# DeltaNet and an MLP on one core: the first MLP product in 15 block products instead of 11 of 12, joins on four tiles, and a new planned order

## The chip, the cores and the metric

The kernel runs on one core of a Trainium2 chip. Its time is the device time of that core in microseconds (us), the median over the runs. A core has five engines, each with an in-order queue: PE (TensorE matmuls; their weight loads are listed apart as PEld), DVE (VectorE), ACT (ScalarE), POOL (GpSimd) and SP (SyncE, which here only issues DMAs). POOL issues DMAs too.

## The reference

All in float32, with B = 4, H = 8, S = 768, D = 48:

```python
k_n = k / (norm(k) + 1e-6)
state = zeros((B, H, D, D))
for t in range(S):                                   # DeltaNet, per batch and head
    y[:, :, t] = einsum('bhd,bhde->bhe', q[:, :, t], state)
    v_old = einsum('bhde,bhd->bhe', state, k_n[:, :, t])
    state += beta[:, :, t] * einsum('bhd,bhe->bhde', k_n[:, :, t], v[:, :, t] - v_old)
x = y.transpose(0, 2, 1, 3).reshape(B, S, H * D)     # (4, 768, 384)
xn = (x - mean) / sqrt(var + 1e-6) * g_ln
out = x + maximum(xn @ w_ch1, 0) @ w_ch2             # 384 -> 1536 -> 384
```

## The kernel before, in words

*Chunks.* The sequence is cut into 12 chunks of 64 steps. Within a chunk the recurrence becomes matrix work for all 32 (batch, head) pairs: Gram matrices of the keys, the inverse of a triangular 64x64 matrix per pair, and then products with the state. After the recurrence of chunk c (`recur`) its 256 tokens (64 steps of 4 batches) go through LayerNorm and the MLP (`mlp(c)`). The chunks depend on each other through the state alone; the MLPs are free to lag behind.

*Inverse.* `rows_inverse` treats two chunks at once. The Gram matrix goes out to DRAM (tile `gd`), comes back by eight DMAs as `gb` with one 32x32 block per partition, is inverted row by row on DVE into `xb` (two operations per row, L1045 and L1050, over the scratch tile `tmp`), goes out to DRAM again (`xd`), and comes back by eight DMAs as the diagonal blocks of `xt`. Chunk 1 has 16x16 blocks and an extra step, `blocks_join` (L1077, L1082: 128 small products, matrices of 32 rows and 32 columns at four positions of the array). Then `join(c)` makes the off-diagonal 32x32 block of each 64x64 inverse: a transposed copy `xnj` on DVE, product E (L1110), a negated copy `es` on ACT, product Z (L1115), and a copy into `xt` on ACT. Each product is 32 matmuls, alternating between two positions of the array; the copies are two of 512 columns.

*Recurrence.* Per chunk PE makes the products with the keys and queries (L963), the state's products (L1160), u (L1215), y (L1222) and the state's update (L1232), each about 1 us. The turn of y into tokens, the LayerNorm and the transposes into `xnt` follow.

*MLP.* The first product is 384 -> 1536 for 256 tokens, the second 1536 -> 384. Chunks 0, 1 and 2 (c < FROM = 3) make the first product plainly: 12 tiles of three matmuls of 256 columns (L1483). From chunk 3 on it goes through `eleven`: with the inputs in three blocks, the hidden units in two halves, and the tokens in two halves, 11 block products replace 12. Each block product is three slabs of two matmuls of 128 columns (L1416). It needs five mixes of token blocks per chunk on POOL (L1397) and, once, sums of blocks of the weights on POOL (`sums_of_w1`, L1372), three into the buffers `q_` and two in place. DVE adds the PSUM banks into the hidden tiles (L1438), ACT copies and applies relu (L1432, L1435). The second product from chunk 1 on is `seven`: 7 block products in place of 8 (L1584), with combinations of the hidden blocks on POOL (L1570, L1609). Filler products on zeros (L1662) keep PE busy where nothing else is ready at the start.

*Order.* Nothing runs where it is written. Each operation is recorded as a Step with a cost, the buffers it reads and writes, and a priority; a list scheduler (class `Line`, `run`) plans start times with modelled costs, and every engine's queue is then issued in the planned order. MLP products on PE carry a due time, taken from a table:

```python
DUE = [44.40, 70.70, 90.32, 129.22, 162.45, ...]     # one entry for each chunk, then slopes
def due(c, t): return DUE[c] + DUE[12 + min(c, 2)] * t
```

A product with a due time yields to small recurrence work unless its due time is close (URGENT, STALL). HOP, GIVE, PATIENCE, SLACK and EAGER are further constants of the planner. The order in which the parts are recorded breaks ties:

```python
prep_x(1); mlp(0); ...; prep_g(2); prep_x(2)
for c in range(2, NCH):
    step(c)                  # loads, norms, queries, join, recurrence of chunk c
    mlp(c - 1)
    if c % 2 and c + 3 < NCH: prep_g((c + 3) // 2); prep_x((c + 3) // 2)
mlp(NCH - 1)
```

All DMAs go through one helper (L555), on SP's queue or on POOL's.

Of the kernel before, what the change touches and what calls it, by code (L numbers as in the profile page):

```python
# [16 lines left out]
C = 64  # L17
DP = 64
# [47 lines left out]
PASS = 0.0165  # L66


class Step:
    __slots__ = (  # L70
        "eng", "cost", "fn", "deps", "pr", "lag", "bulk", "start", "end", "n", "users", "name", "t0", "np", "arr", "hold", "ready", "least", "due", "port", "banks"
# [3 lines left out]
class Line:  # L75
# [17 lines left out]
    def add(self, eng, cost, fn, r=(), w=(), pr=0.0, lag=0.0, bulk=None, name="", t0=0.7, after=(), np=0, arr=0.0, hold=None, due=None, port=0):  # L93
# [3 lines left out]
        s.hold, s.due = False, due  # L97
# [137 lines left out]
    def run(self):  # L235
# [47 lines left out]
        while todo:  # L283
            best = None
            for e in ENGS:
                for rd, s in self.avail[e]:
                    t = when(s, e, rd)
                    if t is not None and (best is None or t < best[0]):
                        best = (t, e)
# [4 lines left out]
            t, e = best  # L294
# [32 lines left out]
            s.start = t  # L327
            if e in ports:
                ports[e] = (t + s.cost, s.port)
# [3 lines left out]
            if s.bulk is not None:  # L333
                free[e] = t + s.cost
                self.dma_go(t)
                self.sent["sw" if e == "Pool" else "hw"].append(s)
                self.rings[e].append([s, max(s.bulk, 1e-6), t + s.cost + self.DMA_ISSUE])
                continue
# [5 lines left out]
            else:  # L344
                free[e] = s.end = t + s.cost
# [10 lines left out]
    def schedule(self):  # L356
# [5 lines left out]
        for s in reversed(every):  # L362
# [3 lines left out]
            s.pr = min(late + [s.due if s.due is not None else 1e6])  # L366
# [31 lines left out]
def kernel(  # L398
# [47 lines left out]
    NH = 14  # L446
# [46 lines left out]
    half_w = DFF // 2  # L493
    second = [t.rearrange("p h t -> p (h t)") for t in (qts[1], pts[1])]
    q_ = [second[0][:, 0:half_w], second[1][:, 0:half_w], sb("q_last", [128, half_w])]
    d_ = [t[:, half_w + 128 * i : half_w + 128 * i + 128] for t in second for i in range(2)] + [ident]
# [258 lines left out]

    def fill(n, cols, ps, pk, after=(), **kw):
# [257 lines left out]
    def rows_inverse(L, chunks, beta_l, xd, **kw):  # L1014
        gv, xv = (t.rearrange("p s t -> p (s t)")[:, 0 : L * L].rearrange("p (s t) -> p s t", t=L) for t in (gb, xb))
        gbk = [("gb", n) for n in range(8)]
        nb, ns = GH * L, 13.7 if L == BK else 11
        add("Pool", 0.1 + 0.85e-3 * L * L, lambda: nc.gpsimd.memset(xv, 0.0), [], ["xb"], after=MASK_SCRATCH, **kw)
        for n, (p0, c, rows, cols) in enumerate(spots(L, chunks)):
            dma(  # L1020
                "SP", gv[p0 : p0 + GH], gds[c % NG][rows, :, cols].rearrange("s h t -> h s t"),
                nb, ns, [("gd", c % NG)], [("gb", n)], **kw,
# [11 lines left out]
        add("Pool", 0.25, lambda: nc.gpsimd.tensor_copy(out=diag(xv), in_=db), ["db_b"], ["xb"], **kw)  # L1034
# [5 lines left out]
        for j in range(L - 1):  # L1040
            n, w = j + 1, L - 1 - j

            def row(j=j, n=n, w=w):
                t = tmp[:, 0 : n * w].rearrange("p (s t) -> p s t", t=w)
                nc.vector.tensor_tensor(  # L1045
                    out=t, in0=xv[:, 0:n, j : j + 1].to_broadcast([128, n, w]),
                    in1=gv[:, j : j + 1, j + 1 : L].to_broadcast([128, n, w]), op=ALU.mult,
                )
                rest = xv[:, 0:n, j + 1 : L]
                nc.vector.tensor_tensor(out=rest, in0=rest, in1=t, op=ALU.subtract)  # L1050
# [3 lines left out]
        dma("SP", xdv, xv, 128, 25 + L * L * 0.15, ["xb"], [("xd", xd)], **kw)  # L1054
        for n, (p0, c, rows, cols) in enumerate(spots(L, chunks)):
            if L < BK:
# [3 lines left out]
                nb, ns, [("xd", xd), ("xz", c % NX)], [("xq", c % NX, n % 8 if L < BK else n % 4)], **kw,  # L1060
            )

    def blocks_join(c, **kw):
# [5 lines left out]
        XN, ES = ([(n, 0), (n, 1)] for n in ("xn", "es"))  # L1069
# [14 lines left out]
        pe(128, prod_e, gk + XN, ATT, 0.22, **kw)  # L1084
        add("ACT", act(512), lambda: nc.scalar.mul(es, pe_, -1.0), ATT, ES, **kw)
        pe(128, prod_z, ES + xq + XT, BY[:2], 0.22, **kw)
# [6 lines left out]
    def xt_keys(c):  # L1093
        return [("xq", c % NX, n) for n in range(8)] + [("xz", c % NX)] + [
            (n, c % NX, g) for n in ("xt", "xo") for g in range(2)
        ]

    def join(c, **kw):
# [7 lines left out]

        def prod_e():
            for h in range(GH):
                for e in range(2):
                    nc.tensor.matmul(p[quad(2 * e + 1), h], gs[quad(2 * e), h, BK:C], xnj[quad(2 * e), h])  # L1110

        def prod_z():
            for h in range(GH):
                for e in range(2):
                    nc.tensor.matmul(p[quad(2 * e), h], es[quad(2 * e + 1), h], xt[quad(2 * e + 1), h, c0 : c0 + BK])  # L1115

        pe(64, prod_e, gk + [("xn", 0), ("xn", 1)], [ATT[1]], 0.11, name=f"e{c}", **kw)
        for e in range(2):
            rows = quad(2 * e + 1)
            add("ACT", act(512), lambda rows=rows: nc.scalar.mul(es[rows], p[rows], -1.0), [ATT[1]], [("es", e)], **kw)  # L1120
        pe(64, prod_z, [("es", 0), ("es", 1)] + xq, [ATT[0]], 0.11, name=f"z{c}", **kw)
        for e in range(2):
            rows = quad(2 * e)
            add(
                "ACT", act(512), lambda rows=rows: nc.scalar.copy(xt[rows, :, BK:C], p[rows]),
                [ATT[0]], [("xo", c % NX, e)], **kw,
# [678 lines left out]
```

## Time and profile before

| what | value |
|---|---|
| median of 3 runs | 560.05 us (558.03 to 564.31) |
| span of the profiled execution | 559.0 us, 1.05 below the median of the runs |
| busy: PE / DVE / ACT / POOL | 525.5 / 370.3 / 192.1 / 253.2 us |
| first product, chunks 3 to 11 (L1416) | 648 matmuls of 128x128 |
| second product, chunks 1 to 11 (L1584) | matmuls of 128x192 |
| PE idle up to 175 us / from there to 460 us | 26 us / about 3 us |

A row of the timeline reads: start, length, engine, line, operation, output and inputs by the program's names, tile shape and count; a bracket at its end is the idle time of the engine just before, and what ended it. PE's counts in the timeline are records, of which a float32 matmul has two. A row of the groups has shapes, count, busy time, mean ns of one, and idle time before.

### The profile page before, as it was taken

To read this page: it belongs to the slowest core of one execution; us is meant where nothing else is said; L and a number is where in the kernel's file an instruction comes from. 1 tells how busy PE (TensorE), PEld (TensorE's weight loads), DVE (VectorE), ACT (ScalarE), POOL (GpSimd) and SP (SyncE) were. 2 spreads that over 40 slices of the span, in tenths; PEclk is the share of its full clock that TensorE was granted. 3 is DMA by queue.
4 is the path that set the end of the run, shared out by engine and by line. 5 is a ranking of instruction groups with operands and counts; after the bars stand their busy time and mean duration, and the time that the engine had idled before them with its cause. 6 is when DMAs were issued, how large, how long until landed. Compare 5 with 4: busy or idle time off the path is not lost.

```text
span 559.0 us, 23060 instructions
## 1 busy us (share of the span) xinstructions
PE 525.5 (94%) x10060; PEld 478.8 (86%) x10060; DVE 370.3 (66%) x884; ACT 192.1 (34%) x452; POOL 253.2 (45%) x399
## 2 busy tenths in 40 slices
PE   7668869899998999899999999999999999999996
PEld 4547657678987899899999999999999999999996
DVE  5666549991689936889858968668777436253331
ACT  5667644232232324232323332513322224323030
POOL 5252337407885656267270352452352522426242
PEclk9898899999998999899999999999999999999999
DMA  9784784269454786553652543834404410111101
GB/s 177 265 158 128 195 219 64 44 149 168 55 86 71 139 195 86 106 100 83 162 77 50 99 81 77 191 46 81 94 15 103 106 30 33 32 48 40 28 1 28
DMA packets 195972, 54.65 MB, mean 98 GB/s; under 512 B 186136, under 2 KB 189344, under 8 KB 195872
## 3 DMA queue, kind: packets, MB, share of 16 engines
q1 hardware_dynamic: 190112, 40.39, 37.8%
q10 hardware_dynamic: 3552, 9.63, 5.0%
q0 software_dynamic: 2208, 3.17, 3.2%
q8 instruction: 78, 1.28, 1.0%
q14 instruction: 22, 0.18, 0.1%
HBM read 36.38 MB, written 16.78 MB: 95 GB/s over the span
## 4 chain that ended last, share of the span: by engine, by line
PE 78%; DVE 7%; DMA 6%; SPq 4%; issue 2%; ACT 1%; POOL 0%; DVEq 0%; POOLq 0%; ACTq 0%
PE f L1584 28%; PE f L1416 25%; PE f L1483 6%; SPq L555 4%; PE two L963 4%; DVE xb L1050 2%; DVE tmp L1045 2%; PE by L1222 2%; PE two L1215 2%; PE by L1160 2%; PE two L1160 2%; DMA gd<-gsb 2%; PE two L1232 2%; PE f L1505 1%; PE by L1115 1%
## 5 line engine op out<-in xcount | busy, mean ns | idle before, releaser
L1584 PE MATMUL f<-w_sb,h_all 128*128 128x192 f32 x396 | 95.0, 332 | 0.0
L1584 PE MATMUL f<-words,h_all 128*128 128x192 f32 x396 | 93.1, 328 | 0.0
L1570 POOL TENSOR_TENSOR h_all<-h_all 128x256 f32<-128x256 f32 x99 | 73.0, 742 | 43.3 <-PE f L1584 37.1
L1416 PE MATMUL f<-xnt,w_sb 128*128 128x128 f32 x648 | 88.8, 279 | 0.0
L1609 POOL TENSOR_TENSOR words<-h_all 128x128 f32<-128x128 f32 x66 | 30.3, 472 | 121.0 <-ACT h_all L1435 101.5
L1416 PEld LDWEIGHTS f<-xnt,w_sb 128*128 128x128 f32 x648 | 81.0, 193 | 0.7
L1438 DVE TENSOR_TENSOR h_all<-f,h_all 128x256 f32<-128x256 f32 x135 | 56.5, 421 | 34.1 <-PE f L1416 20.2
L1050 DVE TENSOR_TENSOR xb<-xb,tmp 128x60 f32<-128x60 f32 (+19 forms) x170 | 73.4, 432 | 5.8
L1045 DVE TENSOR_TENSOR tmp<-xb,gb 128x60 f32<-128x60 f32 (+19 forms) x170 | 65.3, 384 | 7.1 <-POOL xb L1034 4.5
L1584 PEld LDWEIGHTS f<-words,h_all 128*128 128x128 f32 x396 | 68.3, 190 | 0.4
L1584 PEld LDWEIGHTS f<-w_sb,h_all 128*128 128x128 f32 x396 | 66.4, 190 | 1.6 <-issue 0.2
L1483 PE MATMUL f<-xnt,w_sb 128*128 128x256 f32 x216 | 51.7, 390 | 0.0
L1483 PEld LDWEIGHTS f<-xnt,w_sb 128*128 128x128 f32 x216 | 41.3, 195 | 7.2
L555 POOL DMA_DIRECT2D tb<-in_k_dram x64 | 41.7, 656 | 7.0 <-DVE kt L943 5.8
L1602 DVE TENSOR_TENSOR o<-f,x 128x192 f32<-128x192 f32 x33 | 11.7, 355 | 47.7 <-PE f L1584 28.4
L1435 ACT ACTIVATE h_all<-f 128x256 f32<-128x256 f32 x54 | 20.6, 381 | 53.8 <-PE f L1416 28.0
L1584 PE MATMUL f<-w_sb,words 128*128 128x192 f32 x132 | 32.5, 330 | 0.6 <-DVE o L1602 0.6
L1602 POOL TENSOR_TENSOR o<-o,words 128x192 f32<-128x192 f32 x22 | 13.3, 624 | 38.6 <-DVE words L1602 38.6
L1492 ACT ACTIVATE h_all<-f 128x256 f32<-128x256 f32 x36 | 13.8, 383 | 38.2 <-PE f L1483 38.0
L1435 ACT ACTIVATE h_all<-h_all 128x256 f32<-128x256 f32 x54 | 22.2, 413 | 11.3 <-DVE h_all L1438 11.2
L748 POOL TENSOR_TENSOR w_sb<-words 128x768 uint32<-128x768 uint32 (+1 forms) x11 | 14.9, 1356 | 24.3 <-ACT words L738 19.4
L825 POOL TENSOR_TENSOR v<-v,knrm 128x768 f32<-128x768 f32 x11 | 16.7, 1518 | 16.7 <-DMA v<-in_v_dram 16.0
(235 smaller groups left out, 941.3 us busy)
## 6 DMA issues: line engine op xcount, KB each, us to landing
words<-in_moe_w_ch_dram ACTq DMA_DIRECT2D x10, 768.0 KB, 7.2
gd<-gsb SPq DMA_DIRECT2D x11, 512.0 KB, 3.9
v<-in_v_dram SPq DMA_DIRECT2D x24, 192.0 KB, 4.2
out_dram<-o SPq DMA_DIRECT2D x48, 96.0 KB, 2.3
kr<-in_k_dram SPq DMA_DIRECT2D x46, 96.0 KB, 3.0
xld<-xlt SPq DMA_DIRECT2D x9, 384.0 KB, 3.7
xnt<-xld SPq DMA_DIRECT2D x36, 96.0 KB, 3.0
gb<-gd SPq DMA_DIRECT2D x40, 64.0 KB, 3.7
```

What stands on the lines that cost most here:

```text
L555: add(eng, cost, lambda: QUEUE[eng].dma_start(out=out_, in_=in_), r, w, bulk=n * ns / 16e3, **kw)
L963: nc.tensor.matmul(pair[hp][half(e ^ (hp & n)), (g * NP + j) * C : (g * NP + j + 1) * C], kt[drows(hp), l], rt[drows(hp), i],)
L1045: nc.vector.tensor_tensor(out=t, in0=xv[:, 0:n, j : j + 1].to_broadcast([128, n, w]), in1=gv[:, j : j + 1, j + 1 : L].to_broadcast([128, n ...
L1050: nc.vector.tensor_tensor(out=rest, in0=rest, in1=t, op=ALU.subtract)
L1416: nc.tensor.matmul(wide(p[:, 128 * n : 128 * n + 128]), w[:, f : f + 128], r, start=start and n == 0, stop=stop, skip_group_check=True)
L1435: add("ACT", act(256), lambda: nc.scalar.activation(to[0], p, ACTF.Relu), pk, to[1])
L1438: add("DVE", dve(256), lambda: nc.vector.tensor_tensor(out=to[0], in0=ps(p), in1=y[0], op=op), [*pk, *y[1]], to[1])
L1483: nc.tensor.matmul(p[:, 0:TOK], w1_sb[:, t, f * 128 : (f + 1) * 128], xnt[:, t], start=(t == 0), stop=(t == KC - 1))
L1570: add(eng, cost, lambda: e.tensor_tensor(out=out_, in0=x, in1=y, op=op), r, w, port=2 if eng == "Pool" else 1, pr=-2)
L1584: lambda f=f, t=start and f == 0: nc.tensor.matmul(p[:, 0:D2], lhs(f), rhs[:, f], start=t, stop=(f == F2 - 1), skip_group_check=True),
L1602: lambda: e.tensor_tensor(out=out_, in0=a, in1=b_, op=ALU.add), r, w, pr=pr,
L1609: lambda f=f + i: e.tensor_tensor(out=s3[f], in0=one(0, 0)[0](f), in1=one(1, 0)[0](f), op=ALU.subtract),
```

## The change

What it does, by parts:

- `fifteen` takes the place of `eleven`: inputs, and hidden units, in three blocks, tokens in two; 15 block products replace 18. A block product is four matmuls of 128 columns into one of four PSUM banks A to D, 60 matmuls for a chunk. It takes ten mixes of token blocks per chunk on POOL, five of them in place in `xnt` or the mixed buffers. Sums of the weights: 14 on POOL and 2 on DVE, each of 512 columns, eight of them in place in `w1_sb`, once, before the first use. Sums and copies out of PSUM are of 512 columns.
- `join` uses four positions of the array per product instead of two, and four copies of 256 columns on ACT instead of two of 512.
- `rows_inverse` for chunks 4 and 5 (`spare=True`) uses the tiles `pts[1]` and `qts[1]` in place of `gb` and `xb`. The two operations of a row become two Steps, so that other work on DVE can stand between them.
- `state_up` uses 48 instead of 64 columns of weights from chunk 1 on. `seven` takes the f-tiles of its second product in another order. `h_all` holds 12 tiles instead of 14.
- The planner: other constants and due times, a table CAP of latest times for u and the xt loads, a cost of POOL and DVE sharing (OVERLAP), ties broken by engine time.

The diff, cut:

```diff
-    HOP, GIVE, PATIENCE, SLACK, EAGER = 0.17, 0.1, 0.8, 3.0, 0.0
+    HOP, GIVE, PATIENCE, SLACK, EAGER = 0.17, 0.0, 0.033, 3348.957, 0.345
...
-    URGENT, STALL = 6.0, 0.25
-    PE_TAIL, SWITCH = 0.12, 0.1
+    URGENT, STALL = 6.0, 0.288
+    PE_TAIL, SWITCH, OVERLAP = 0.12, 0.1, 0.1
...
-                    if t is not None and (best is None or t < best[0]):
+                    if t is not None and (best is None or (t, max(free[e], rd)) < best[:2]):
...
-    NH = 14
+    NH = 12
...
-    def rows_inverse(L, chunks, beta_l, xd, **kw):
-        gv, xv = (t.rearrange("p s t -> p (s t)")[:, 0 : L * L]... for t in (gb, xb))
+    def rows_inverse(L, chunks, beta_l, xd, spare=False, **kw):
+        own = (pts[1]..., qts[1]...) if spare else (t... for t in (gb, xb))
...
-            add("DVE", 2 * dve(n * w), row, gbk, ["xb"], port=1, **kw)
+            add("DVE", dve(n * w), <tmp = column * row>, [*gbk, xbk], ["tmp"], port=1, **kw)
+            add("DVE", dve(n * w), <rest -= tmp>, ["tmp"], [xbk], port=1, **kw)
...
         def prod_e():
-            for h in range(GH):
-                for e in range(2):
-                    nc.tensor.matmul(p[quad(2 * e + 1), h], gs[quad(2 * e), h, BK:C], xnj[quad(2 * e), h])
+            for j in range(H):
+                for e, g in spread_:
+                    h = H * g + j
+                    nc.tensor.matmul(p[quad(2 * e + 1 - g), h], gs[quad(2 * e), h, BK:C], xnj[quad(2 * e), h])
...
-        for e in range(2):
-            rows = quad(2 * e + 1)
-            add("ACT", act(512), lambda rows=rows: nc.scalar.mul(es[rows], p[rows], -1.0), [ATT[1]], [("es", e)], **kw)
+        for e, g in spread_:
+            add("ACT", act(256), lambda e=e, g=g: nc.scalar.mul(es[quad(2 * e + 1), heads[g]], p[quad(2 * e + 1 - g), heads[g]], -1.0), ATT, [("es", e, g)], **kw)
...
-    DUE = [44.40, 70.70, 90.32, 129.22, 162.45, 201.63, ...]
+    DUE = [68.885, 68.173, -0.54, 142.635, 655.75, 75.302, ...]
+    CAP = [84.167, 134.541, 352.72, ...]
...
-        for s in range(3):                               # eleven
-            prod(pa, ka, s, W(0, 1), B(1, 1), start=True)
-            copy(h(0, 1), pa, ka)
-            prod(pb, kb, s, W(1, 1), D(0), start=True)
-            sum_(h(0, 0), pb, kb, h(0, 1), ALU.subtract)
...
+        mix(N(0), B(0, 1), B(2, 1), ALU.add)             # fifteen
+        prod("C0", N(0))
+        copy((1, 1), "C")
+        prod("B0", B(1, 1))
+        sum_((1, 1), "B", (1, 1))
+        mix(N(1), B(1, 1), B(2, 1), ALU.add)
+        prod("D0", N(1))
...
-            eleven(c, hs)
-            return seven(c, hs, 33 * 0.43)
+            three = fifteen(c, hs)
+            return seven(c, hs, 30 * 0.448, three)
...
-        rows_inverse(BK, (2 * m, 2 * m + 1), ..., m % 2, pr=pr)
+        rows_inverse(BK, (2 * m, 2 * m + 1), ..., m % 2, spare=m == 2, pr=pr)
```

More of the change, by code (lines that the diff above doesn't have):

```diff
@@ L327, in run @@
             s.start = t
+            cost = s.cost
             if e in ports:
-                ports[e] = (t + s.cost, s.port)
+                until, kind = ports["Pool" if e == "DVE" else "DVE"]
+                if s.port and kind + s.port > 2 and t < until + 1e-9:
+                    cost -= self.OVERLAP
+                ports[e] = (t + cost, s.port)
             todo -= 1
@@ L344, in run @@
             else:
[L345 removed]
+                free[e] = s.end = t + cost
             for b in s.banks:
@@ L491 @@
     eps = sb("eps", [128, 1])
[L493 to L496, printed above, removed]
+    FB4 = DFF // 3
+    more = [t.rearrange("p h t -> p (h t)") for t in (qts[1], pts[1])] + [sb("w_more", [128, 2 * FB4])]
+    w_new = [t[:, FB4 * i : FB4 * i + FB4] for t in more for i in range(2)]
+    x_new = [*(sb(f"x_new{i}", [128, 128]) for i in range(2)), ident]
     st = sb("st", [128, 2, 2, 6])
@@ new lines, in N, with mix, prod, go @@
+        def N(i):
+            return wide(x_new[i]), [("x_new", i)]
+        def mix(o, x, y, op):
+            (o, ok), (x, xk_), (y, yk) = o, x, y
+            add(
+                "Pool", 0.47, lambda: nc.gpsimd.tensor_tensor(out=o, in0=x, in1=y, op=op), xk_ + yk, ok[-1:],
+                after=["ident"] if o is N(2)[0] else (),
+            )
+        t0 = [0.0]
+        banks = {n: fours[fifth[i]] for i, n in enumerate("ABCD")}
+        begun = set()
+        def prod(n, rhs):
+            (w, wk), (r, rk) = form(n), rhs
+            p, pk = banks[n[0]]
+            start = n[0] not in begun
+            begun.add(n[0])
+            for v in range(2):
+                def go(v=v):
+                    for i in (2 * v, 2 * v + 1):
+                        f = 128 * i
+                        nc.tensor.matmul(
+                            wide(p[:, f : f + 128]), w[:, f : f + 128], r, start=start and i == 0, stop=True, skip_group_check=True
+                        )
+                add("PE", 0.448, go, [*wk, *rk], pk, due=due(c, t0[0]), np=4, arr=0.448)
+                t0[0] += 0.448
```

297 lines of the change are left out of this document (170 added, 127 removed).

## The prediction

> **What bounds the kernel now.** I read the busy times first, then the chain that ended last, then busy time by stage. Columns of the stage rows are the length, then busy time and record count of PE, weight loads, VectorE (DVE), ScalarE (ACT) and GpSimd (POOL), the granted clock and DMA.
>
> ```profile
> span 559.0 us, 23060 instructions
> PE 525.5 (94%) x10060; PEld 478.8 (86%) x10060; DVE 370.3 (66%) x884; ACT 192.1 (34%) x452; POOL 253.2 (45%) x399
> PE 78%; DVE 7%; DMA 6%; SPq 4%; issue 2%; ACT 1%; POOL 0%; DVEq 0%; POOLq 0%; ACTq 0%
> ...
> 0.00:66.40 66.40, 49.00 (x1258) 37.79 (x1259) 43.41 (x137) 42.94 (x96) 26.52 (x43) 0.92 0.76 189
> 66.40:130.00 63.60, 56.73 (x1295) 43.07 (x1295) 49.46 (x100) 23.67 (x48) 25.36 (x33) 0.97 0.58 122
> 130.00:165.30 35.30, 34.91 (x594) 31.64 (x592) 19.62 (x44) 11.56 (x27) 30.00 (x47) 1.00 0.61 91
> 165.30:175.00 9.70, 8.10 (x150) 6.44 (x150) 8.69 (x14) 1.66 (x6) 5.43 (x7) 0.84 0.66 111
> 175.00:226.20 51.20, 49.65 (x1190) 43.98 (x1188) 36.97 (x84) 17.07 (x37) 30.79 (x48) 1.00 0.66 126
> 226.20:460.00 233.80, 232.49 (x4326) 223.43 (x4326) 174.26 (x416) 69.63 (x173) 98.72 (x160) 0.99 0.44 88
> 498.70:554.60 55.90, 55.89 (x420) 55.23 (x419) 19.44 (x49) 12.24 (x34) 23.50 (x41) 1.00 0.11 29
> ```
>
> From 175 on, when the MLP of chunk 2 starts, PE is idle for about 3 us in 380 and runs at full clock: every PE microsecond taken out there comes off the end, as long as the others keep up (DVE is busy for 174 of 234). Before 175 PE idles 17.4 in the first stage, 6.9 in the second, and in 165.3 to 175 it mostly runs filler products (L1662). There the chain through DVE and the DMA queues counts, and PE work is worth little.
>
> **Fifteen products for eighteen.** The old scheme does 11 block products of six 128x128 matmuls per chunk, 66; the new one 15 of four, 60. Nothing else of the shape changes: 128 rows, 128 columns of weights, 128 tokens. A matmul shows as two records.
>
> ```profile
> 498.69 13.55 PE f L1416 x120
> ```
>
> ```profile
> 540.71 13.89 PE f L1584 x84
> ```
>
> 120 records in 13.55 us are 0.113 each, with no gaps. Six matmuls are 12 records, 1.36 us a chunk, for chunks 3 to 11: 9 x 1.36 = **-12.2**. Other pitches in the trace hardly differ, so I keep no second bound. Sums and copies out of PSUM become wider and fewer (10 of 128x512 for 18 of 128x256 on DVE, 11 for 18 on ACT), about the same elements in all; both engines have room in the rows above. The second product (84 records, 13.89) is unchanged.
>
> **Joins over four tiles.** A join is two products of 64 records on 32x32 tiles that alternate between two positions. The block join of chunk 1 already goes round four positions, and stands beside them as a measure.
>
> ```profile
> 88.12 1.29 PE L1082 MATMUL by<-xt,es 32*32 32x32 f32 x128
> 89.34 1.56 PE L1483 MATMUL f<-xnt,w_sb 128*128 128x256 f32 x6
> ```
>
> ```profile
> 397.49 1.13 PE by L1110 x64
> ```
>
> ```profile
> L1435 ACT ACTIVATE h_all<-f 128x256 f32<-128x256 f32 x54 | 20.6, 381 | 53.8 <-PE f L1416 28.0 <-DVE h_all L1438 19.5 <-DVE o L1602 2.2
> ```
>
> Start to next start, 128 records take 1.22, so 64 take 0.61, against 1.13: 0.52 saved. Chunks 2 to 11 have 20 such products: **-10.4**. The new order puts two of the four positions on the same 32 rows, which L1082 does not, so the other bound is 0. L1082 is the nearest row in tile size, and I take it. ACT's copies after each become four of 256 columns (0.38 by the last row) in place of two of 512; that lies behind PE's other products, and where that cover is gone (chunk 2, below) it is counted.
>
> A rule speaks against this edit. The Trainium skill (TensorE: Matmul & The Clock Gate, "Wait — 56ns, not 53.3ns?") says that matmuls never start closer than about 25 ns, however small. By it the joins would gain nothing and the sum would be 10.4 higher. The rows above have 9.5 ns a record (19 a matmul), so the trace disagrees.
>
> **State update with 48 columns of weights in place of 64.**
>
> ```profile
> 388.32 0.93 PE two L1232 x64
> ```
>
> ```profile
> 478.94 1.08 PE two L1160 x64
> ```
>
> L1232 takes 0.93 with 64 columns; L1160 takes 1.08 with 48. So narrower isn't shown to be faster: 0, with 48/64 of 0.93, or -2.3 over ten chunks, as the other bound.
>
> **The front, up to the MLP of chunk 2.** Three things move.
>
> ```profile
> 23.46 4.31 SPq L555 DMA_DIRECT2D gb<-gd  x6
> 27.81 2.65 SPq L555 DMA_DIRECT2D kr<-in_k_dram  x4
> 30.50 3.47 SPq L555 DMA_DIRECT2D tb<-in_k_dram  x4
> 34.02 1.12 SPq L555 DMA_DIRECT2D gb<-gd  x2
> ...
> 60.88 6.09 SPq L555 DMA_DIRECT2D gb<-gd  x8
> 67.08 0.42 SPq L555 DMA_DIRECT2D xd<-xb  x1
> 69.37 5.17 SPq L555 DMA_DIRECT2D xt<-xd  x8
> ```
>
> ```profile
> 42.18 1.12 PE L930 MATMUL by<-xt,xt 64*64 64x64 f32 x30 [3.66 <-DVE nrm_b L1028]
> 82.59 1.70 PE L1077 MATMUL f<-xnj,gsb 32*32 32x32 f32 x128 [4.37 <-DVE xnj L1071]
> 140.68 0.72 DVE L1027 TENSOR_SCALAR nrm_b<-nrm_b 128x32 f32<-128x32 f32 x1 [9.17 <-ACT nrm_b L1026]
> 156.22 1.15 PE L1215 MATMUL two<-v,xt 64*64 64x48 f32 x64
> 163.45 1.89 PE L1584 MATMUL f<-w_sb,h_all 128*128 128x192 f32 x10
> 167.64 1.72 DVE L1045 TENSOR_TENSOR tmp<-xb,gb 128x240 f32<-128x240 f32 x1
> 171.24 1.38 PE L1310 MATMUL by<-ident,xln 128*128 128x128 f32 x6 [1.60 <-DVE xln L1278]
> 174.97 1.60 PE L1483 MATMUL f<-xnt,w_sb 128*128 128x256 f32 x6
> ```
>
> First, all eight gb loads now stand ahead of the kr and tb loads on SP. The last two leave 6 us sooner, and the 3.66 that DVE, and PE behind it, waited for the norms made from them goes: -3.7. The eight loads passed leave 1.1 later, and are first used at 43.
>
> Second, the xd write now leaves ahead of most gb loads in place of behind them (it stood until 67.08). But one gd write, with its wait for ACT, and three gb loads still come before the eight xt loads, and PE now has two tiles of chunk 0's MLP ahead of the block join in place of seven. If the xt loads land sooner, the 4.37 wait goes, and some of the 6.9 idle of that stage; if they land when they did (PE at 82.59), PE arrives at about 66.4 + 2.9 + 2.2 = 71.5 and waits 11, which is 6.7 worse, and the 3.7 is lost behind it.
>
> Third, the inverse of chunks 4 and 5 has buffers of its own, so its loads don't stand behind the one before, and DVE's wait of 9.17 goes. It was not on PE's path: PE had chunk 1's MLP to do meanwhile. What it gives is that chunk 4's blocks are ready long before chunk 4. What is late next is chunk 2: in the new order nearly all of chunk 1's MLP stands ahead of the joins of chunks 2 and 3, and after it comes the bare chain. Its length is an estimate: 4.3 for the join (2 x 0.61 and two times four copies of 0.38); from u's product at 156.22 to the turn at 171.24 15.0, less some 5 of inverse rows and transposes such as the one at 167.64, which stood ahead of the norm on DVE and in the new order don't; 3.7 from the turn to 174.97: 18. PE has some 9 of work beside it (two joins, u, y, state and three products of the next chunk at 1.1 each): 9 lost. Before, 9.7 passed from the last product of chunk 1 (165.3) to 174.97, with some 3.1 of use: 6.6 lost. That is +2.4.
>
> The front is thus between -3.7 - 6.9 + 2.4 = -8 and +6.7 + 2.4 = +9. The waits that the new SP order removes are sure, the other is not, so I take **-4**.
>
> **Work added off PE.** Mixing tokens takes 10 POOL operations a chunk for 5 (0.46 each); sums of the first weights are 14 on POOL and 2 on DVE for 10.
>
> ```profile
> L1397 POOL TENSOR_TENSOR ident<-xnt 128x128 f32<-128x128 f32 x9 | 4.1, 457 | 3.4 <-ACT xnt L1304 3.1 <-PE f L1416 0.3
> L1372 POOL TENSOR_TENSOR w_sb<-w_sb 128x384 f32<-128x384 f32 x4 | 4.1, 1017 | 4.3 <-PE f L1483 4.3
> 158.66 1.62 POOL L825 TENSOR_TENSOR v<-v,knrm 128x768 f32<-128x768 f32 x1
> 158.98 1.54 DVE L1050 TENSOR_TENSOR xb<-xb,tmp 128x220 f32<-128x220 f32 x1
> 211.51 2.57 POOL L555 DMA_DIRECT2D tb<-in_k_dram  x4
> ```
>
> A sum of 512 columns is 1.36 by L1372's width. The eight in place come after chunk 2's last first product, with six combinations at 0.74: 15.3 on POOL, against 13.9 of second products and 5 of recurrence on PE. Hidden, with some 4 to spare; if that cover is gone, up to 11 is lost once. I take 0.
>
> **Sum.** 559.0 - 12.2 - 10.4 - 4 = 532.4 of span. The median of the runs (560.05) lies 1.05 over the span: **533.5**.
>
> **Rivals.** *The front gets worse*: PE's wait for the block join grows to 11, and the front ends at +9: 546.5. For it: the xt loads run beside the loads of weights, and PE meets them with five tiles less behind it. Against: the xd write leaves ahead of the gb loads.
>
> *The four tiles don't overlap*, because they share rows in pairs: 544. For it, no 32-wide row of the trace shares rows; against, L1232, whose four 64-wide tiles share rows in pairs and whose 64 records take only 0.93. (The skill's 25 ns rule ends in the same place.)
>
> *POOL holds DVE*: at 158.66 a POOL sum ran, and the DVE row beside it took 1.54 where its neighbours take 0.40. 45 added mixes at 0.46 are 20.6; if all of it reached PE through late sums, 554. Against: DVE has 60 us to spare between 226 and 460. The Trainium skill (SBUF — State Buffer, "SBUF: two separate sides") has an exclusive port pair for such pairs of operations; the two rows agree.
>
> *Slower*: the mixes feed PE's in-order queue, and POOL is in order too. A mix that stands behind four k loads (2.57) or a v scaling (1.62) holds PE as long. The new order does place some mixes behind such issues. At 2.57 + 1.62 less some 0.5 of cover it is 3.7 a chunk, 33 in all: 567. It decides from 3 us a chunk, where the gain of 26.6 is gone. Against: three products, 2.7 us, usually lie between a mix and its use, and the k loads end well before the last chunks.
>
> **Chances.** Forecast 0.62; its own range is 527 (front -8, state update -2.3) to 540 (front 0, and 2.5 of late sums). Front worse 0.13; no overlap 0.11; POOL holds DVE 0.06; slower 0.08. The range reaches up over the next two rivals and down by 4 more of the first stage's 17.4 idle, of which I took 3.7: 523 to 547. A measurement here tells about 1% from no change, 554.4 to 565.7. Faster holds the first three and half of the fourth, 0.89; same the other half, 0.03; slower 0.08.
>
> **What would show it.** Right: 120 records of the first product a chunk at 0.113; join products of 64 records in about 0.6; the MLP of chunk 2 starting near 171; PE idle under 5 us after it. Wrong: joins still at 1.1; a wait at the block join over 8; PE waits before first products with POOL as releaser; or the MLP of chunk 2 starting later than 175.

## The result and the profile after

The changed kernel takes 550.03 us in the median (548.37 to 553.89), the kernel before 560.41 (558.03 to 564.31): a ratio of 0.9858, 95% interval 0.9815 to 0.9900. A second set of runs gave 0.9889 (0.9834 to 0.9944). It is faster, by 1.1 to 1.4%, where 4.7% was predicted; 550.03 lies outside the range of 523 to 547. The profiled execution has a span of 546.7, so 12.3 of the 26.6 predicted came.

The page of the changed kernel, with the line of the queue that carries PE's instructions:

```profile
span 546.7 us, 22861 instructions
...
PE 506.7 (93%) x9950; PEld 456.3 (83%) x9950; DVE 366.8 (67%) x814; ACT 209.8 (38%) x460; POOL 287.1 (53%) x457
...
q8 instruction: 78, 1.28, 1.0%
```

PE is busy for 18.8 less, and idle for 6.5 more. Busy time by stage, up to the start of chunk 2's MLP (174.5) and behind it, and then the two last stages of the kernel before:

```profile
0.00:66.40 66.40, 50.55 (x1372) 40.25 (x1373) 46.03 (x139) 45.53 (x99) 28.95 (x45) 0.87 0.80 190
66.40:130.00 63.60, 57.28 (x1183) 43.63 (x1183) 46.12 (x102) 22.75 (x51) 27.16 (x36) 0.95 0.64 124
130.00:174.50 44.50, 40.07 (x733) 35.04 (x731) 36.65 (x84) 13.18 (x39) 28.12 (x43) 0.96 0.59 94
...
174.50:487.20 312.70, 304.76 (x6275) 284.84 (x6268) 216.86 (x449) 112.67 (x242) 174.40 (x282) 1.00 0.45 90
487.20:546.70 59.50, 54.08 (x410) 52.58 (x401) 21.12 (x42) 15.71 (x30) 28.48 (x53) 0.98 0.13 34
```

```profile
175.00:487.50 312.50, 309.64 (x6280) 293.49 (x6281) 224.85 (x527) 98.20 (x237) 138.51 (x225) 0.99 0.45 90
487.50:559.00 71.50, 67.09 (x506) 66.38 (x498) 24.25 (x63) 14.04 (x39) 27.36 (x47) 0.99 0.11 29
```

The front is 0.5 shorter (174.5 for 175.0; predicted 6.1, with the four joins that lie in it). Behind it the time falls from 384.0 to 372.2, by 11.8 (predicted 20.5): busy time 17.9 less, idle time 6.1 more. The recurrences take as long as before (312.7 and 312.5); the gain shows in the MLP that is left when they end. The waits of PE, the longest ones:

```profile
PE by L1098 <- issue: 4.5, 1, 4.5
PE two L937 <- issue: 2.9, 2, 2.2
PE f L970 <- issue: 2.2, 1, 2.2
PE f L1562 <- issue: 2.0, 1, 2.0
PE two L970 <- issue: 1.9, 4, 0.7
PE two L922 <- issue: 1.9, 1, 1.9
PE f L1093 <- DVE xnj L1087: 1.7, 1, 1.7
```

Before, the longest were DVE's xnj (4.37), the norms (3.66) and u (2.17). Those are gone or short, as forecast. In their place stand waits called issue, in which nothing that the profile shows is late: 17.8 in all, wait by wait, against 4.7 before (one of those is the 1.55 at 223.7 that the prediction passed over). They are odd in that they stop PE in the middle of a product:

```profile
73.68 1.05 PE L1098 MATMUL by<-xt,es 32*32 32x32 f32 x101
79.22 0.64 PE L1098 MATMUL by<-xt,es 32*32 32x32 f32 x27 [4.48 <-issue]
...
174.50 1.56 PE L1562 MATMUL f<-xnt,w_sb 128*128 128x256 f32 x6
```

After 101 of its 128 records the block join's second product stands still for 4.48. Counted over all of PE's records, the waits stand at numbers 221, 475, 856, 983, 1619, 3149, 3788, 4043, 4171 and so on: the differences are multiples of 128, short by a few where records are missing. The instruction queue made 78 fetches for 9950 records, one for 127.6. So the supply theory: PE's instructions come in blocks of 128 records, the next block is asked for when PE crosses into the last one, and a run of small products uses a block up sooner than the next one lands. The planner in the code has it too (`BLOCK, FIRST, FETCH = 128, 93, 3.95`, a line of the diff's surroundings): a fixed 3.95 us for a block. The rival is the order theory: the small products are as cheap as their rows say, and the new planned order lost the rest by waits of its own.

The Trainium skill (Runtime: NRT & Kernel Launch, "Instruction fetch mechanics") has the same blocks, 16 KiB or 256 instructions, and says that the cost of crossing from one to the next is mostly hidden. The 128 matmul records and 128 weight loads of a block agree with it; the 17.8 us of waits do not.

### The profile page after: what moved, and what is told of

Same layout as the page of the kernel before. It is cut to its first block, busy times and chain, and to the rows that moved or that the text cites. A ratio compares the mean times of both kernels' runs of the same rounds, so it can differ in the third digit from the quotient of the medians.

```text
span 546.7 us, 22861 instructions
## 1 busy us (share of the span) xinstructions
PE 506.7 (93%) x9950; PEld 456.3 (83%) x9950; DVE 366.8 (67%) x814; ACT 209.8 (38%) x460; POOL 287.1 (53%) x457
## 5 line engine op out<-in xcount | busy, mean ns | idle before, releaser
L1486 DVE TENSOR_TENSOR h_all<-f,h_all 128x512 f32<-128x512 f32 x72 | 49.1, 686 | 25.4 <-PE f L1463 22.8
L1481 ACT COPY h_all<-f 128x512 f32<-128x512 f32 x45 | 26.2, 585 | 86.4 <-PE f L1463 73.3
L1059 DVE TENSOR_TENSOR tmp<-xb,gb 128x31 f32<-128x31 f32 (+19 forms) x139 | 57.0, 410 | 3.1
L1066 DVE TENSOR_TENSOR xb<-xb,tmp 128x31 f32<-128x31 f32 (+19 forms) x139 | 57.3, 412 | 2.6
L1562 PEld LDWEIGHTS f<-xnt,w_sb 128*128 128x128 f32 x216 | 40.6, 194 | 9.0 <-issue 2.8
L1490 ACT ACTIVATE h_all<-h_all 128x512 f32<-128x512 f32 x54 | 33.7, 630 | 32.0 <-DVE h_all L1486 31.5
L1463 PE MATMUL f<-x_new,w_sb 128*128 128x128 f32 x288 | 41.9, 278 | 0.8 <-POOL x_new L1446 0.8
L1463 PE MATMUL f<-xnt,w_sb 128*128 128x128 f32 x288 | 42.0, 277 | 0.0
L1463 PEld LDWEIGHTS f<-x_new,w_sb 128*128 128x128 f32 x288 | 37.4, 192 | 1.6 <-POOL x_new L1446 1.1
L1463 PEld LDWEIGHTS f<-xnt,w_sb 128*128 128x128 f32 x288 | 37.7, 192 | 0.3
L1571 ACT ACTIVATE h_all<-f 128x256 f32<-128x256 f32 x36 | 13.7, 383 | 46.0 <-PE f L1562 39.3
## 6 DMA issues: line engine op xcount, KB each, us to landing
xld<-xlt SPq DMA_DIRECT2D x9, 384.0 KB, 2.9
```

The source lines that it names most:

```text
L1059: lambda j=j, n=n, w=w, t=t: nc.vector.tensor_tensor(out=t, in0=xv[:, 0:n, j : j + 1].to_broadcast([128, n, w]), in1=gv[:, j : j + 1, j + ...
L1066: "DVE", dve(n * w), lambda t=t, rest=rest: nc.vector.tensor_tensor(out=rest, in0=rest, in1=t, op=ALU.subtract),
L1463: nc.tensor.matmul(wide(p[:, f : f + 128]), w[:, f : f + 128], r, start=start and i == 0, stop=True, skip_group_check=True)
L1481: add("ACT", act(512), lambda: nc.scalar.copy(o, p), pk, ok)
L1486: add("DVE", dve(512), lambda: nc.vector.tensor_tensor(out=o, in0=x, in1=y, op=op), [*xk_, *yk], ok)
L1490: add("ACT", act(512), lambda: nc.scalar.activation(o, o, ACTF.Relu, scale=scale), [], ok)
```

## The experiments

Each experiment edits the changed kernel and keeps its planned order, unless it says otherwise. "Behind" is the time from the start of chunk 2's MLP to the end; the front is the time up to that start. Each ratio is to the kernel before, measured along with the run.

**E1, joins two at a time.**

```diff
+        turns_ = [(g, j, e) for g in range(2) for j in range(H) for e in range(2)]
...
-            for j in range(H):
-                for e, g in spread_:
+            for g, j, e in turns_:
```

> The changed kernel in its own order, with one edit: inside the two products of a join the matmuls again alternate between two positions of the array, not four. Supply theory: PE gets its instructions in blocks (every wait called issue in the changed kernel stands about 128 records after the one of the block before), and a block cannot come sooner than about 4.1 us after the one ahead of it was begun; faster joins run into that edge. The 20 products go back from 0.68 to 1.13 us (+9.0), but waits called issue shrink from 17.9 by 2 to 4, so the span grows by 5 to 7, to about 552 to 554. Order theory: the joins pay in full and what was lost lies in the new order; the issue waits stay at 17.9 and the span grows by 9, to about 556.

Measured: 557.05, ratio 0.9955 (0.9914 to 0.9995); span 556.2; behind, 376.6. A product takes 1.04, not 1.13, so going back costs 16 x 0.36 = 5.8 behind, of which 4.5 shows. The issue waits behind did not shrink (5.5 for 5.6), against the supply theory's expectation: the sum of 21.7 is larger by the front alone, which differs from run to run (E5). So most of the joins' own length shows here, and making them slower, with as many instructions, does not take the waits away.

**E2, the kernel before with four positions.** Kernel before, its own order; the first of the two products (`eg(g)` is g, and 0 for chunk 5):

```diff
-            for h in range(GH):
-                for e in range(2):
-                    nc.tensor.matmul(p[quad(2 * e + 1), h], gs[quad(2 * e), h, BK:C], xnj[quad(2 * e), h])
+            for e, g, j in turns_(c != 5):
+                    h = H * g + j
+                    nc.tensor.matmul(p[quad(2 * e + 1 - eg(g)), h], gs[quad(2 * e), h, BK:C], xnj[quad(2 * e), h])
...
```

> The kernel before in its own order, with 18 of the 20 join products on four positions of the array (the E product of chunk 5 and the Z product of chunk 4 stay on two) and ACT's copies in halves. Order theory: 18 x 0.45 = 8.1 less, a span of about 551, issue waits unchanged at 4.7. Supply theory: issue waits grow by 2 to 4, and the gain is 4 to 6, a span of 553 to 555.

Measured: 556.15, ratio 0.9934 (0.9900 to 0.9969), a gain of 3.7 where 8.1 was the full price. A product fell from 1.13 to 0.68 as in the changed kernel. The issue waits rose from 4.7 to 10.2, but 4.1 of that stands ahead of the first join. The row behind (length first):

```profile
176.00:557.70 381.70, 371.72 (x6773) 353.67 (x6772) 251.28 (x592) 117.15 (x310) 166.52 (x272) 0.99 0.39 79
```

381.7 for 384.0: 2.3 of 14 x 0.45 = 6.3. PE is busy for 5.0 less there (371.7 for 376.7) and idle for 2.7 more, 0.75 of it in issue waits. So even without the new order less than half of the joins' price arrives.

**E3, the supply by itself.** A program of its own, one profile; its core, with 32x32 tiles at four positions (the remarks are added here):

```python
full(128, f[0], bb)    # 128 matmuls of 128x128
four(640, f[1], bb)    # 640 of 32x32 on four positions
two(640, f[2], bb)     # 640 on two positions
```

> PE alone, nothing of the reference is computed: 128 matmuls of 128x128, 640 small ones on four positions, 640 on two positions, then 64 large ones, 640 small ones on four positions while 12 writes to DRAM of 64-element rows run, and 128 large ones. Supply theory: 128 records of small matmuls take about 4.1 us in the steady state on four and on two positions alike, though they run in about 1.4 and 2.3 where the instructions are there, with a pause at each edge; more than 4.1 (up to 7) while the DMAs run; no pause in the large ones. Order theory: 1.4 and 2.3 us for 128 records throughout, with or without DMAs.

```profile
37.66 1.93 PE L41 MATMUL f<-b,a 32*32 32x32 f32 x128 [2.10 <-issue]
41.38 1.93 PE L41 MATMUL f<-b,a 32*32 32x32 f32 x128 [1.80 <-issue]
45.11 1.92 PE L41 MATMUL f<-b,a 32*32 32x32 f32 x128 [1.80 <-issue]
...
70.11 18.26 PE L47 MATMUL f<-b,a 32*32 32x32 f32 x640 [0.26 <-issue]
...
155.68 30.97 PE L51 MATMUL f<-y,a 128*128 128x128 f32 x256
```

On four positions PE stops every 128 records, for 1.5 to 2.3 us, and starts a new block every 3.45 to 3.73 (3.36 and 4.00 at the ends). The clock does not set this: most of it ran at a granted clock of 0.5, and the two periods at full clock, which end at 37.66 and 125.27, are 3.36 and 3.56. On two positions 128 records take 3.65 as well, but without the expected stop at each edge; at half clock PE's own pace may set that, and this run does not tell the two apart. The large products run without a stop. By the packets of the instruction queue a period is 1.1 from crossing an edge to the start of the fetch, 0.9 to 1.4 for the fetch, and 1.4 from its end to PE's next instruction. The order theory has no place for the stops. The DMAs had ended near 122, just as the second set of small products began, so what they do stayed open (E11).

**E4, the state's update on 64 columns.** `w = DP` in place of `D if c else DP`.

> The changed kernel in its own order, with the state's update on 64 columns of weights again. One update goes from 0.83 to 1.04 us, ten of them 2.1. Order theory: span 546.7 + 2.1 = 548.8. Supply theory: a little less, 547 to 548.5, because some updates stand before a block's edge that waits anyway.

Measured: 553.92, ratio 0.9900 (0.9856 to 0.9943); behind, 374.3 for 372.2: +2.1. An update goes from 0.83 to 1.04, and eight of the ten lie behind: 8 x 0.21 = 1.7, which 2.1 meets within the 0.4 by which two profiles of one kernel differ there (E5). So here the full length arrives, as the order theory has it, though one of the eight updates stands at an edge (record 6584).

**E5, the changed kernel again.** No edit.

> The changed kernel once more, for a second profile beside the three below. Supply theory: the waits called issue stand at the same records as in the first profile (93 to 56 records past a multiple of 128); those before 130 us, where the DMA engines are busy, differ by 1 to 3 us from run to run, those after 175 hardly. Order theory: the same waits of the same lengths.

Measured: 554.27, ratio 0.9889; span 555.2; behind, 372.6, as in the first profile. Of the 8.5 between the two profiles 8.1 lies in the front:

```profile
66.40:130.00 63.60, 56.06 (x1154) 41.07 (x1153) 38.47 (x88) 20.65 (x45) 23.64 (x29) 0.86 0.57 112
130.00:182.60 52.60, 48.85 (x764) 42.94 (x762) 40.82 (x96) 15.24 (x44) 31.70 (x49) 0.90 0.60 94
```

The granted clock (third number from the end) is 0.86 and 0.90 for 0.95 and 0.96. It comes in stretches of 3.4 us at full or half speed; before chunk 2's MLP starts 48 us are at half speed here, 27 in the first profile, 17 in the kernel before. PE's idle time in the front is nearly the same in the two profiles (27.1 and 26.6); what differs is that PE is busy for 7.6 longer. The waits stand on the same series of record numbers, with other lengths in the front (2.5 in place of 0.7 at record 856, 1.1 in place of 4.5 at 1619, some gone and some new) and the same lengths behind, within 0.4. E4 and E6 to E8 have this front too, but for the few small matmuls of E6 to E8. Chunk 2's MLP starts at 177.3 to 181.1 in them, with 34 to 38 us at half speed, so the first profile, with 174.5, is the earliest of six.

**E6, E7, E8, the edges moved.** 16, 32 or 48 small matmuls on zeros near the start:

```diff
+            for i in range(extra):
+                a = quad(i % 4)
+                nc.tensor.matmul(ps[a, 32 * (i // 4) : 32 * (i // 4) + 32], nought[a, 0:32], nought[a, 0:32])
```

> The changed kernel in its own order, with 16 matmuls of 32x32 on zeros (32 records, about 0.3 us, while PE waits for its first loads) added near the start, which only move the edges of the instruction blocks. Supply theory: the issue waits move to other instructions, 32 records earlier in the stream, and their sum changes by some us, up or down (it is 17.9 in the first profile); the span moves with it. Order theory: the same waits at the same instructions, span unchanged within 1 us.

> As the run with 32, with 32 matmuls (64 records, about 0.5 us). Supply theory: the issue waits stand 64 records earlier in the stream than in the changed kernel, and their sum is another one. Order theory: the same waits at the same instructions.

> As the run with 32, with 48 matmuls (96 records, about 0.8 us). Supply theory: the issue waits stand 96 records earlier in the stream; the last of them after 175 us, which end with edges just behind a run of small products, shrink or grow by up to 2 us each. Order theory: the same waits at the same instructions.

Measured: 549.72 (0.9818, 0.9772 to 0.9865), 556.85 (0.9932, 0.9897 to 0.9966) and 552.72 (0.9865, 0.9803 to 0.9928). The waits keep to the same series of record numbers (221, 475 or 476, 856 or 857, 983, 1619 and 3788 in all three), and so fall on other instructions. With 32 more, record 3788, in the changed kernel a key product with 0.35 of wait, is the state's product with the queries:

```profile
195.44 0.47 PE L1186 MATMUL by<-s_all,qt 48*64 48x48 f32 x8 [2.56 <-issue]
```

The sums are 15.2, 17.5 and 19.6. This decides where the waits stand: they belong to the record's number, not to the instruction. The time behind (371.4, 371.6, 370.7) hardly depends on where the edges fall.

**E9, E10, fewer instructions.** Each of the block join's two products, and each join product up to chunk 3 in E9 and of all chunks in E10, becomes one matmul of 512 columns. It mixes blocks that the join keeps apart, so these two kernels leave out the right inverse; the order and all other operations stay. One of the edits:

```diff
         def prod_e():
+            if c < 4:
+                return nc.tensor.matmul(bank, gs[:, 0:2].rearrange("p h t -> p (h t)"), xnj.rearrange("p h t -> p (h t)"))
```

In E10 the condition is `if True:`.

> The changed kernel in its own order, but the two products of the block join of chunk 1 and those of the joins of chunks 1 to 3 are each one matmul of 128x128 by 512 columns into the same bank (two records in place of 128 or 64; the inverses are then not those of the reference). PE's own time hardly falls: about 0.95 us in place of 1.22 or 0.68, so 2 x -0.27 + 6 x 0.27 = +1. What falls is the number of instructions, by 2 x 126 + 6 x 62 = 624 records, five blocks of 128. Supply theory: the waits called issue before 175 us fall from 9 to 12 us to under 7, fewer stretches run at half clock, and the MLP of chunk 2 starts 3 to 8 us sooner than the 174.5 to 182.6 of the changed kernel. Order theory: the same waits at the same instructions, and the front 1 us longer.

> As the run before, for the joins of all chunks (22 products of 62 records less each, and the block join's two). After 175 us PE gets 16 x 0.27 = 4.3 us more to do and 990 records less to fetch. Supply theory: the issue waits after 175 us fall from 5.6 to under 3, so that stage grows by 1 to 3 only, and the front is as in the run before. Order theory: +4.3 after 175 us and +1 before.

Measured: E9 544.81 (0.9700, 0.9636 to 0.9763), E10 541.68 (0.9627, 0.9578 to 0.9675). In E9 the MLP of chunk 2 starts at 172.83, 1.7 sooner than in the first profile and 9.8 sooner than in the second, where 3 to 8 was expected. From the first stage to there it has no issue wait, but 8.9 are left within the first stage, where under 7 was expected. Behind, it takes 371.9, as the changed kernel. E10's rows, waits and the stage behind:

```profile
PE two L937 <- issue: 3.8, 2, 2.6
PE two L970 <- issue: 1.1, 1, 1.1
PE two L922 <- issue: 1.1, 1, 1.1
```

```profile
173.10:479.90 306.80, 304.04 (x5279) 279.44 (x5276) 218.99 (x452) 112.98 (x242) 174.14 (x282) 1.00 0.45 91
```

The issue waits behind fall from 5.6 to 1.5, and 366.3 is left of 372.2, although the joins there cost PE 2.9 more by their starts (14.4 for 11.5). PE is busy for 1.7 more than in the changed kernel over the whole, and the span is 7.3 shorter (the median 8.4): the number of instructions binds there, not PE's time in them. The granted clock behind is 1.00 in both. The expectation had the sign wrong (+1 to +3 behind, -5.8 measured): besides the 4.1 of issue waits, other idle time falls by 1.1, and PE's unchanged products take some 3.5 less from start to start.

**E11, the supply while DMAs run.** As E3, with 16 large matmuls in place of 64 ahead of the last small ones, and the writes in rows of 16.

> PE alone as in the first run of this kind, but the 12 writes to DRAM are in rows of 16 elements, so that they last while the last 640 small matmuls run (nothing of the reference is computed). Supply theory: without them 128 records every 3.45 to 3.73 us, as measured; while they run 5 to 7.5 us, with the added time between the crossing of an edge and the start of the fetch. If the DMAs do not matter: 3.7 throughout.

```profile
116.89 1.93 PE L41 MATMUL f<-y,a 32*32 32x32 f32 x128 [4.03 <-issue]
121.99 1.93 PE L41 MATMUL f<-y,a 32*32 32x32 f32 x128 [3.17 <-issue]
125.72 1.93 PE L41 MATMUL f<-y,a 32*32 32x32 f32 x128 [1.80 <-issue]
```

The DMAs ended near 123, so two blocks saw them: 5.29 and 5.10 in place of 3.36 to 4.00, with 2.9 and 2.7 in place of 1.1 between the crossing and the fetch. In the first profile of the changed kernel the periods that end in a wait before 80 us, with the DMA engines 0.8 busy, are 5.4 to 7.3, and behind 175 us mostly 3.7 to 5.0.

**E12, the old plan.** HOP to STALL and DUE of the kernel before, no CAP.

> The changed kernel's operations, planned with the constants and due times of the kernel before (no caps). Order theory: the new tables cost time, and with the old ones the gain comes out: 535 to 545. Supply theory: the old tables know nothing of where the edges fall now; more issue waits than the 18 of the changed kernel, and a time of 555 to 570.

Measured: 567.84, ratio 1.0138 (1.0084 to 1.0192). The new tables do not cost time; with the old ones the same operations are 14 to 18 slower. But the issue waits were 8.0, not more than 18: this order loses by late xnj (4.9), o (4.3) and mixes (3.1). Supply is not all that an order can lose by, and the number of records alone does not make the waits either: this order issues 1352 records in the first 66.4 us (1372 in the changed kernel) without one issue wait. Its front ends at 173.0; what it loses lies behind.

**E13, E14, a norm behind two relus.** Of the front's issue waits 4.5 us stand at one place, 73 to 79. There ACT's norm of the next inverse also waits, ahead of two relus of the MLP. The changed kernel's ACT, and SP's queue ahead of it:

```profile
77.32 0.26 ACT L1038 ACTIVATE nrm_b<-gb 128x32 f32<-128x32 f32 x1 [4.29 <-DMA gb<-gd]
...
77.48 0.64 ACT L1571 ACTIVATE h_all<-f 128x256 f32<-128x256 f32 x2
```

```profile
62.35 6.25 SPq L559 DMA_DIRECT2D xt<-xd  x8
68.64 2.60 SPq L559 DMA_DIRECT2D gb<-gd  x5
71.29 4.75 SPq L559 DMA_DIRECT2D ksum<-gd  x2
```

The xt loads leave 7 us sooner than before (69.37), and five gb loads and the ksum loads now stand behind them. E9 had shown that the two waits stand in one place: without the issue wait PE waits 5.06 there for the relu.

```profile
77.00 2.90 PE L1561 MATMUL f<-xnt,w_sb 128*128 128x256 f32 x6 [5.06 <-ACT h_all L1570]
```

With this edit the norm and what follows it come up to 4 us later in the order, in E14 with E9's products:

```diff
+    for s in line.steps:
+        if 470 <= s.n <= 538 and s.start < 90.05:
+            s.start = 74.0 + 0.8 * (s.start - 70.05)
```

> The changed kernel, in which the inverse of chunks 2 and 3 (its norm on ACT, L1038, and the row operations on DVE behind it) is put up to 4 us later in the order: behind two relus of chunk 0's MLP on ACT and behind the block join's copy on DVE. In the changed kernel the norm stands ahead of them and waits for its last gb load until 77.3. Theory that both waits stand in the same place: PE's wait inside the block join's second product (4.5 us in the profile, an instruction block) is there in any case, so the front gains 0 to 2. Theory that the norm alone holds PE: the wait of 4.5 goes, and the front gains 4.

> The run with coarse products up to chunk 3 (624 records fewer) together with the later norm. There PE waits 5.06 for ACT at 77.0 and for no instruction block. Theory that both waits stand in the same place: with both taken away that wait is under 2, and the MLP of chunk 2 starts near 168 to 170, in place of 172.8. If PE waits for something else there: no change.

Measured: 552.75 (0.9887, 0.9784 to 0.9990) and 551.05 (0.9836, 0.9738 to 0.9934): no gain in either, and E14, slower than E9 (0.9700), did not meet its expectation: chunk 2's MLP starts at 178.2 in it. ACT and PE of E14 show why:

```profile
84.17 0.21 ACT L1166 ACTIVATE knrm<-ksum 128x16 f32<-128x16 f32 x1 [10.09 <-DMA ksum<-gd]
...
85.21 0.36 ACT L1570 ACTIVATE h_all<-f 128x256 f32<-128x256 f32 x1
```

```profile
85.62 2.93 PE L1561 MATMUL f<-xnt,w_sb 128*128 128x256 f32 x6 [7.50 <-ACT h_all L1570]
```

The next operation that waits for a passed load, ksum, now holds the next relu, and PE waits 7.50 for it. So the front has a second bound beside the supply: loads that the xt loads were moved ahead of, and ACT's order behind them.

**E15, E16, E17, other orders.** The same operations, planned with longer blocks (5.8, 4.3, 3.9 us by stage in E15; 5.0, 4.1, 3.9 in the others) and slower DMAs, due times and constants searched anew.

```diff
-                    lo = begun + self.FETCH if bi else 0.0
+                    lo = begun + (5.0 if begun < 125.0 else 4.1 if begun < 240.0 else 3.9) if bi else 0.0
```

> The changed kernel's operations in another planned order: the planner reckons with 5.8 us for a block of PE's instructions before 125 us, 4.3 up to 240 and 3.9 behind it (3.95 throughout in the changed kernel) and with slower DMAs while many run, and its due times and constants are chosen anew under that. Theory that instruction blocks and late loads took the missing gain: waits called issue under 10 us (18 and 15 in the two profiles of the changed kernel) and a time of 538 to 548. If they are not what binds, the new order gives 548 to 556, as the changed kernel.

> As the run before, with milder assumptions: 5.0, 4.1 and 3.9 us for a block and a smaller slowing of the DMAs, and due times chosen anew under these. The same two expectations: issue waits under 10 us and 538 to 548, or 548 to 556.

> The assumptions of the run before, with due times that another search found. Expected as there; it shows how much of the result is the search's luck.

Measured: 583.42 (1.0432, 1.0355 to 1.0509), 548.14 (0.9784, 0.9702 to 0.9865) and 555.52 (0.9930, 0.9887 to 0.9973). The issue waits were 17.7, 19.7 and 14.8, nowhere under 10. E16 has the lowest median of the kernels with all operations, though its interval overlaps the changed kernel's. Its gain is in the front:

```profile
168.35 1.46 PE L1562 MATMUL f<-xnt,w_sb 128*128 128x256 f32 x6
```

Chunk 2's MLP starts 6.2 sooner; behind it 373.5 are left, 372.2 in the changed kernel. That a plan with longer blocks makes fewer waits is not borne out. E16 and E17 plan with the same assumptions and end 7 us apart, so much of a search's result is luck; E15, with the longest blocks and slowest DMAs, is 28 slower than either.

## Why the prediction was wrong

*Fifteen products: right.* 12 records of the new product take 1.34 from start to start, 0.112 each; 108 fewer behind 175 are -12.1, predicted -12.2. The busy time of the whole line there, in which overlap with its neighbours counts too, fell by 14.2 (147.3 to 133.1). In the table before the prediction the 648 are records, of one group of that line alone; it has 1188, which are 594 matmuls, 66 a chunk.

```profile
276.86 1.50 PE L1463 MATMUL f<-x_new,w_sb 128*128 128x128 f32 x12
278.20 0.82 PE L1662 MATMUL f<-words,h_all 128*128 128x192 f32 x4
```

*Joins: right in kind, too high.* In the rows below, 186.81 to 187.50 is 0.69 for 64 records, where 0.61 was read off the block join, so about 0.45 each and -9.0 for -10.4. By the busy time of all 16 behind 175 (19.2 to 12.6) it is 0.41 each. The four positions overlap although they share rows in pairs; that rival fell, and with 11 ns a record, 22 a matmul, the trace again disagrees with the floor of about 25 ns that the Trainium skill gives (TensorE: Matmul & The Clock Gate, "Wait — 56ns, not 53.3ns?").

```profile
186.81 0.75 PE L1130 MATMUL f<-xnj,gsb 32*32 32x32 f32 x64
187.50 0.68 PE L1183 MATMUL by<-s_all,qt 48*64 48x48 f32 x32
```

*State update: the other bound was nearer.* 0 was taken, about -2 came (E4).

*The front: the step that failed first.* "The front, up to the MLP of chunk 2" was to give -4, and -6.1 with its joins; it gave -0.5 in the first profile and +7.6 in the second. The waits it named did go: nrm_b 3.66 to 0.33, xnj 4.37 to 1.71. But PE's idle time in the front stayed as it was, 26.6 and 27.1 in the two profiles for 26.3 before, because the issue waits there rose from 3.2 to 12.2 and 9.6; the sum had no term for them. Two more things were left out. Of the moved xd and xt loads it priced the xt loads alone, not the gb and ksum loads that they passed, nor ACT's relus that stand behind the operations on those (E13, E14). And it took the front at the clock of the kernel before: 27 and 48 us are at half speed for 17. With that goes nearly all of the 8.1 between the two profiles (PE busy for 7.6 longer, E5); what lowers the clock is not shown. How the loss in the front divides among the three stays open.

*The sum behind 175: the step that failed second.* "Every PE microsecond taken out there comes off the end" does not hold where instructions are late. PE's idle time there was to stay under 5; up to its last product it is 8.1, for 2.9 before. The issue waits rose from 1.55 to 5.6; E10 gets them back to 1.5 by fewer instructions. The busy time fell by 17.9. By the lines' own busy time, the terms above made -22.3 with the state's update, and products that were not changed took 4.8 more: the second product 3.2, the key products 1.0, chunk 2's plain first product 0.7. The second product before, after and in E10 (busy time of PE behind the length):

```profile
175.00:559.00 384.00, 151.02 (x840) 134.73 (x840) 0.99 0.39 78
174.50:546.70 372.20, 154.19 (x840) 134.34 (x840) 1.00 0.40 81
173.10:539.40 366.30, 153.60 (x840) 134.89 (x840) 1.00 0.40 82
```

In E10 the three take 1.7 less than in the changed kernel, so a part of the 4.8 goes with the number of instructions too; for the rest I have no cause.

*The rivals.* POOL holds DVE, and mixes stuck behind POOL's queue, did not come: the one wait for a mix in the first profile is 0.8. "Front worse" named the xt loads' landing as its cause, and the block join did start at 70.97 as its early case had it; the loss came from the issue waits and from what was passed. None of the rivals was an instruction block, though the profile of before had the 1.55 wait and the code the constant.

## What to carry to other kernels

A wait called issue in the middle of a product is worth counting: if PE's record numbers at such waits differ by multiples of one constant, the engine waits for instructions. Making small products shorter can then gain less than their length (E2), and making them fewer can gain more than PE's time in them (E10). The number of records alone does not say how much, for another order of the same operations had 1.0 of these waits in the front in place of 12.2 (E12). When a group of loads is moved forward in a queue, price every load that it passes, and whatever stands in order behind the operations on those. A front that differs by 8 us between two profiles of one kernel needs more than one profile before a small term of it is believed.

## What the hardware showed that I had not expected

PE alone, with nothing else on the chip's queues, did not run small float32 matmuls at four positions faster than 128 records in 3.36 to 4.00 us (E3). While the DMA engines are full a block takes 5.1 to 5.3 in the small program (E11) and 5.4 to 7.3 in the first profile of the kernel, nearly all of the difference ahead of the fetch. The clock in the front differs between runs of one order: 27 us at half speed in one profile of the changed kernel and 48 in another, for 17 in the kernel before; no run here shows why.
